# Windowed attention and SwiGLU on one core: fixed instruction orders, loads that cast, DMA transposes

## The chip, the cores and the metric

The kernel runs on one core of a Trainium2 chip. The metric is device time in microseconds (us), lower is better. Engines are named as in the profile: PE (matmuls; PEld its weight loads), DVE, ACT, POOL, and the queues SPq, ACTq and POOLq from which DMAs are issued. PSUM is the memory that PE writes its results to. The granted clock (row PEclk) is the share of PE's full clock that the profile shows. A casting load is a DMA that turns fp32 into fp16 on its way.

## The reference

```
scores = q @ k.T / sqrt(64)            # 8 sequences x 8 heads, 576 tokens, head size 64
scores = where(|i - j| <= 32, scores, -1e9)
x      = softmax(scores) @ v           # laid out as 4608 tokens x 512
out    = (silu(x @ w_gate) * (x @ w_val)) @ w_out      # 512 -> 1536 -> 512
```

Inputs and output are fp32; the kernels compute in fp16 with fp32 accumulation. Queries are taken in blocks of 64, each against 128 keys; a **pair** is two blocks (128 tokens, 36 pairs), its "scores" are the product with K and its "AV" the product with V, a **chunk** is 512 tokens (9 chunks), and a **stage** below is one chunk's FFN1 (12 units of 8 matmuls) and the FFN2 after it (48 matmuls) with four pairs of attention.

## The kernel before

The attention output of a pair is turned by PE and copied by DVE:

```python
def pair_xt(m):
    tp = ps_o.tile([128, GS, 128], FP16, tag="o", name="xt_ps")
    for g in range(GS):
        nc.tensor.transpose(out=tp[:, g, :], in_=x16[:, 128 * g:128 * g + 128], identity=ident)
    ...
    nc.vector.tensor_copy(out=xts[j][:, :, 128 * i4:128 * i4 + 128], in_=tp)
```

Weights come in fp32 slabs that ACT, DVE and POOL cast. The order within an engine is chosen by the compiler's scheduler.

## Time and profile before

| | before |
|---|---|
| time, median of 2 runs | 414.88 us |
| span of the profiled run | 413.3 us |
| first FFN1 matmul | 56.1 us |
| one steady stage, FFN1 start to FFN1 start | 38.85 us |
| PE busy | 358.0 us |

In the slices, each digit is a fortieth of the span. The prediction below shows those of PE, ACT and DMA, the chain of waits of the startup and one steady FFN2. One more pair of rows matters later: the copies of turned Q and K in before, from the page's groups (columns: line, engine, operation, out<-in, shapes, count, then busy us and mean ns of one, then idle time before).

```profile
L275 ACT ACTIVATE kT_106<-qk_ps 128x576 f16<-128x576 f16 x16 | 10.4, 648 | 7.9 <-DMA qst<-in_q_dram 6.4
L273 DVE COPY qB_109<-qk_ps 64x576 f16<-64x576 f16 x16 | 11.9, 744 | 2.8 <-PE qk_ps L267 2.7
```

A copy of 576 elements per partition takes 0.65 us on ACT and 0.74 us on DVE: 1.1 and 1.3 ns an element.

### The profile page before, as it was taken

What the parts mean: (1) busy time and instruction counts of PE and PEld (TensorE: products, weight loads), DVE (VectorE), ACT (ScalarE), POOL (GpSimd) and SP (SyncE); (2) the same over time, 40 slices, a digit from 0 to 9 for tenths busy, and PEclk for the clock granted to TensorE, in tenths of its full rate; (3) what the DMA queues carried; (4) which work ended last, traced back from release to release, by engine and by line L of the source; (5) the groups of instructions that cost most, each with busy time, mean ns of one, the idle gap of its engine ahead of it and who ended that gap; (6) DMA issues with size and microseconds to landing.
All of it is one profiled execution on the core that took longest, in us unless ns stands there. A gap on an engine that the chain in (4) does not pass through costs nothing.

```text
span 413.3 us, 6739 instructions
## 1 busy us (share of the span) xinstructions
PE 358.0 (87%) x2690; PEld 191.5 (46%) x2690; DVE 204.5 (49%) x338; ACT 173.0 (42%) x238; POOL 123.2 (30%) x181
## 2 busy tenths in 40 slices
PE   1210689958999999999999999999999999999994
PEld 0210544454546455554555555555455544544441
DVE  7332634664566464646646564566454633533300
ACT  2321335471455446344633373455436343533321
POOL 4562562856126231622353334133110000000000
PEclk9999999988999999999999999999999999999999
DMA  8999995975333523523363351301100100110022
GB/s 208 259 334 322 245 329 144 166 171 116 114 115 102 152 77 112 153 84 115 109 168 92 85 148 54 116 0 52 52 0 9 71 26 1 52 53 0 26 103 82
DMA packets 61862, 47.70 MB, mean 115 GB/s; under 512 B 39296, under 2 KB 55680, under 8 KB 61824
## 3 DMA queue, kind: packets, MB, share of 16 engines
q1 hardware_dynamic: 58880, 42.87, 38.3%
q10 hardware_dynamic: 2944, 4.33, 3.6%
q8 instruction: 23, 0.38, 0.4%
q14 instruction: 15, 0.12, 0.1%
HBM read 37.75 MB, written 9.44 MB: 114 GB/s over the span
## 4 chain that ended last, share of the span: by engine, by line
PE 78%; DMA 7%; ACT 6%; DVE 5%; SPq 2%; issue 1%; ACTq 0%
PE gv_ps L348 45%; PE ob L362 20%; DMA wst_t<-in_moe_w_gate_dram 5%; PE o_ps L314 4%; PE qk_ps L267 4%; ACT p_t L302 3%; PE s_ps L296 3%; PE xt_ps L332 3%; DVE p_t L305 1%; DMA qst<-in_q_dram 1%; SPq L233 1%; ACT ssb L354 1%; DVE xT L337 1%; ACT osb L370 1%; ACT L302 1%
## 5 line engine op out<-in xcount | busy, mean ns | idle before, releaser
L355 DVE TENSOR_TENSOR hT<-ssb,gv_ps 128x512 f16<-128x512 f16 x108 | 74.3, 688 | 101.6 <-ACT ssb L354 100.3
L354 ACT ACTIVATE ssb<-gv_ps 128x512 f16<-128x512 f32 x108 | 64.5, 597 | 128.4 <-PE gv_ps L348 128.4
L348 PE MATMUL gv_ps<-xT,wg_133 128*128 128x512 f16 x432 | 113.2, 385 | 0.9 <-DVE xT L337 0.5
L348 PE MATMUL gv_ps<-xT,wv_134 128*128 128x512 f16 x432 | 111.7, 381 | 0.0
L362 PE MATMUL ob<-wo_135,hT 128*128 128x512 f16 x432 | 102.0, 379 | 0.5 <-ACT osb L370 0.5
L348 PEld LDWEIGHTS <-wv_134 128*128 128x128 f16 x432 | 42.5, 98 | 51.6 <-issue 1.4
L348 PEld LDWEIGHTS <-wg_133 128*128 128x128 f16 x432 | 41.2, 99 | 46.2 <-issue 3.2
L362 PEld LDWEIGHTS <-hT 128*128 128x128 f16 x432 | 39.6, 98 | 40.4 <-issue 0.6
L370 ACT ACTIVATE osb<-ob 128x512 f32<-128x512 f32 x36 | 21.5, 596 | 55.4 <-PE ob L362 55.4
L257 POOL CAST v_122<-vS 64x512 f16<-64x512 f32 (+1 forms) x52 | 33.7, 648 | 29.7 <-PE o_ps L314 16.1
L257 POOL CAST v_112<-vS 64x512 f16<-64x512 f32 (+1 forms) x52 | 33.1, 638 | 30.8 <-PE o_ps L314 20.1
L302 ACT ACTIVATE p_t<-s_ps 128x1024 f16<-128x1024 f32 x36 | 36.7, 1025 | 12.7 <-PE s_ps L296 10.9
L305 DVE TENSOR_TENSOR p_t<-p_t,mask 128x1024 f16<-128x1024 f16 x36 | 28.1, 779 | 26.8 <-ACT p_t L302 26.6
L314 PEld LDWEIGHTS <-p_t 128*64 128x64 f16 x576 | 19.2, 117 | 14.2 <-issue 5.8
L337 DVE COPY xT<-xt_ps 128x512 f16<-128x512 f16 x36 | 15.1, 419 | 19.9 <-PE xt_ps L332 19.7
L296 PE MATMUL s_ps<-qB_109,kT_106 128*128 128x128 f16 x144 | 13.7, 239 | 10.9 <-ACT kT_106 L275 10.2
L296 PEld LDWEIGHTS <-kT_106 128*128 128x128 f16 x144 | 10.5, 108 | 14.5 <-ACT kT_106 L275 11.0
L314 PE MATMUL o_ps<-v_112,p_t 128*64 128x66 f16 x288 | 12.7, 209 | 3.6 <-DVE x_342 L323 1.2
L314 PE MATMUL o_ps<-v_122,p_t 128*64 128x66 f16 x288 | 11.8, 201 | 3.9 <-DVE x_793 L323 1.3
L296 PE MATMUL s_ps<-qB_119,kT_116 128*128 128x128 f16 x144 | 12.4, 232 | 2.7 <-ACT p_t L302 1.7
L275 ACT ACTIVATE kT_106<-qk_ps 128x576 f16<-128x576 f16 x16 | 10.4, 648 | 7.9 <-DMA qst<-in_q_dram 6.4
L273 DVE COPY qB_109<-qk_ps 64x576 f16<-64x576 f16 x16 | 11.9, 744 | 2.8 <-PE qk_ps L267 2.7
(348 smaller groups left out, 271.8 us busy)
## 6 DMA issues: line engine op xcount, KB each, us to landing
qst<-in_q_dram SPq DMA_DIRECT2D x32, 288.0 KB, 3.2
out_dram<-osb SPq DMA_DIRECT2D x36, 256.0 KB, 2.1
kst<-in_k_dram SPq DMA_DIRECT2D x28, 288.0 KB, 3.4
vS<-in_v_dram SPq DMA_DIRECT2D x24, 256.0 KB, 4.3
vS<-in_v_dram SPq DMA_DIRECT2D x16, 192.0 KB, 4.3
wst_t<-in_moe_w_val_dram ACTq DMA_DIRECT2D x4, 768.0 KB, 10.1
wst_t<-in_moe_w_gate_dram SPq DMA_DIRECT2D x4, 768.0 KB, 10.1
wost_t<-in_moe_w_out_dram SPq DMA_DIRECT2D x4, 768.0 KB, 8.5
```

What stands on the lines that cost most here:

```text
L257: nc.gpsimd.tensor_copy(out=o, in_=i)
L267: nc.tensor.transpose(out=ps[:, i, 96 * j:96 * j + 96], in_=t16[:, j, :, :], identity=ident[0:96, 0:96])
L296: nc.tensor.matmul(out=s[:, i, 128 * hp:128 * hp + 128], lhsT=kT[b % 2][:, hp, 64 * t:64 * t + 128], rhs=qB[b % 2][:, hp, :, 64 * t:64 * t ...
L302: nc.scalar.activation(out=p.rearrange("p a h q -> p (a h q)"), in_=s.rearrange("p a f -> p (a f)"), func=AF.Exp, bias=0.0, scale=1.0 / fl ...
L305: nc.vector.tensor_tensor(out=p, in0=p, in1=mask, op=ALU.mult)
L314: nc.tensor.matmul(out=o[64 * i:64 * i + 64, h // 4, 66 * (h % 4):66 * (h % 4) + 66], lhsT=p[:, i, h, :], rhs=v16[b % 2][:, t, h, :], star ...
L337: nc.vector.tensor_copy(out=xts[j][:, :, 128 * i4:128 * i4 + 128], in_=tp)
L348: nc.tensor.matmul(out=gv[:, i, :], lhsT=w[:, g, 128 * fk:128 * fk + 128], rhs=xts[j][:, g, :], start=(g == 0), stop=(g == GS - 1))
L354: nc.scalar.activation(out=ssb, in_=gv[:, 0, :], func=AF.Silu, bias=0.0, scale=1.0)
L355: nc.vector.tensor_tensor(out=hts[j][:, fk, :], in0=ssb, in1=gv[:, 1, :], op=ALU.mult)
L362: nc.tensor.matmul(out=ob, lhsT=hts[j][:, fk, 128 * sub:128 * sub + 128], rhs=wo16[:, fk, :], start=(fk == 0), stop=(fk == FKS - 1))
L370: nc.scalar.activation(out=osb, in_=ob, func=AF.Copy, bias=0.0, scale=1.0)
```

## The change

The intent: no engine's queue waits for a weight slab, and PE has less to do. Weights, V, and Q and K from the fourth sequence on are cast in the load (issued by POOL); Q and K of those sequences, and x of pairs 8 to 35, are turned by DMA. Q and K of the first three sequences are loaded in long runs and turned by PE. Scores use two half-height row tiles in place of a zero-padded Q. Every engine's order is fixed by hand. The core of it:

```diff
+    PARTS = ((0, 10), (320, 8))
+    fast.enter_context(tc.manual_schedule())
 ...
+    def turn_long(b, part, ks, qs):
+        t0, n = PARTS[part]
+        kd = kT[b % 2][:, :, 32 + t0:32 + t0 + 32 * n].rearrange("c h (p j) -> c j h p", j=n)
+        qd = qT[b % 2][:, :, t0:t0 + 32 * n].rearrange("c h (p j) -> c j h p", j=n)
 ...                                             # casts; n PE transposes for each of K and Q
+            cp(dst, ps[:, 0:n].rearrange("c j (h p) -> c j h p", p=32))
 ...
+    def turn_tok(b, tiles, dst, off):
+        for t0, n, st in tiles:
+            nc.sync.dma_start_transpose(
+                out=dst[:, :, off + t0:off + t0 + n], in_=st[0:n].rearrange("p h d -> p (h d)"))
 ...
-                nc.tensor.matmul(out=s[:, i, 128 * hp:128 * hp + 128], lhsT=kT[...128 rows...], rhs=qB[...128 columns...])
+                    for g in range(2):
+                        nc.tensor.matmul(out=s[:, g, i, hp, :], lhsT=kT[b % 2][64 * g:64 * g + 64, ...],
+                                         rhs=qT[b % 2][64 * g:64 * g + 64, ...])      # 64 columns
 ...
+    def x_dma(ms):
+        for m in ms:
+            x16 = x16s.pop(m).rearrange("p a h d -> p (a h d)")
+            nc.sync.dma_start_transpose(out=x_out(m), in_=x16)
 ...
+    def fetch(b):
+        load_v(b, range(5))                      # POOL: 5 casting loads
+        toks[b] = load_tok(k, b, "k16"), load_tok(q, b, "q16")       # 5 and 5 more
+        for t in (1, 3, 5, 7):
+            shift_v(b, t, cp_pool, cp_pool)
 ...
+    def ffn2(j, pairs):
+        scores(pairs[0:3])
+        ffn2_half(j, 0, 0); ffn2_half(j, 0, 1); ffn2_half(j, 1, 0)
+        avs(pairs[0:2]); scores(pairs[3:4]); x_dma(pairs[0:2])
+        ffn2_half(j, 1, 1); ffn2_half(j, 2, 0)
+        avs(pairs[2:4]); x_dma(pairs[2:4])
+        ffn2_half(j, 2, 1); ffn2_half(j, 3, 0); ffn2_half(j, 3, 1)
 ...
+    for j in range(1, NCH):                      # fetch(b) after unit 0 and place(b), its turning, after unit 9 of FFN1(j > 1)
```

(Lines are cut and joined here; the code is otherwise as in the change.)

## The prediction

> **What bounds the kernel now.** I read the page's slices first, then the chain of waits in order of time, then the timeline of one steady stage engine by engine, then busy time per stretch. The slices:
>
> ```profile
> PE   1210689958999999999999999999999999999994
> ACT  2321335471455446344633373455436343533321
> DMA  8999995975333523523363351301100100110022
> ```
>
> There are two regimes. For five slices (about 56 us) DMA is full and PE nearly idle; after that PE is full and nothing else is above seven tenths for long. The chain tells what the first regime waits for:
>
> ```profile
> 1.28 5.92 DMA qst<-in_q_dram
> ...
> 15.05 11.82 DMA wst_t<-in_moe_w_gate_dram
> 26.90 1.49 ACT wg_133 L251
> 28.41 10.61 DMA wst_t<-in_moe_w_gate_dram
> 39.06 1.36 issue
> 40.43 0.64 ACT kT_106 L275
> 41.12 0.73 PE s_ps L296 x5
> ...
> 56.11 4.27 PE gv_ps L348 x10
> ```
>
> This is the costliest flaw. The copy of the last head pair of K (kT, ACT, 40.43) needs only Q and K, which had landed and were cast by about 15 us. It stands in ACT's in-order queue behind casts of the gate weights, and these wait for 768 KB slabs. So some 25 us pass before the first full score matmul; then four pairs of blocks go through a chain of PE, ACT and DVE with little overlap, and FFN1 starts at 56.11.
>
> The second regime, PE in one FFN2 stage:
>
> ```profile
> 245.30 0.62 PE L296 MATMUL s_ps<-qB_119,kT_116 128*128 128x128 f16 x8
> 245.76 1.46 PE L362 MATMUL ob<-wo_135,hT 128*128 128x512 f16 x6
> 247.06 0.39 PE L332 MATMUL xt_ps<-ident,x_2710 128*128 128x128 f16 x4
> 247.37 0.60 PE L314 MATMUL o_ps<-v_122,p_t 128*64 128x66 f16 x16
> 247.91 1.47 PE L362 MATMUL ob<-wo_135,hT 128*128 128x512 f16 x6
> ```
>
> From start to start (one group's end overlaps the next): scores of a pair cost 0.46 us (8 matmuls), its AV 0.54 us (16, or 34 ns each), its x transposes 0.31 us, and six FFN2 matmuls 1.30 us, or 216 ns each. The chain shows the same 216 ns for FFN1: 80 matmuls in 17.28 us near the end, where nothing is mixed in. Within FFN1 there are also 12 transposes of Q and K per head pair: the timeline of 118 to 120 us has them between 118.63 and 119.14, 0.51 us. A stage of 512 tokens is then 144 x 0.216 = 31.1 us of FFN, 4 x 1.31 = 5.2 us of attention and 4 x 0.51 = 2.0 us of Q/K transposes, 38.3 us; the chain has 38.85 us from one FFN1 start to the next (175.41 to 214.26). So PE has under 1 us of holes per stage, and only less work on PE, or an earlier start, makes this kernel faster. Between 81.05 and 96.7 five pairs of attention stand alone, 15.6 us for 6.6 us of PE work: 9 us lost.
>
> **What the Trainium skill says.** "TensorE: Matmul & The Clock Gate", Part 3 (packing small matmuls), says that matmuls on different row groups run at the same time. The trace of before has no row-tiled matmul; its AV, split over column halves, starts one every 34 ns. "DMA: Bandwidth & Descriptors", SWDGE vs HWDGE vs iDMA, says that only GpSimd-issued DMAs can cast, and that GpSimd cores then compute each descriptor in software; "SBUF — State Buffer", SBUF: two separate sides, adds that some DVE modes lock GpSimd out while it writes them. No run here shows either yet: all loads are hardware queues q1 and q10. "Advanced Engine Details and Errata", X-Bar Transpose (TRN2), says that transposing DMAs are as fast as ordinary ones; not shown yet either.
>
> **The change, part by part.**
>
> *Startup.* Weights and V are cast in the load, so the weight casts leave ACT, DVE and POOL and nobody's queue waits for a slab. Q and K come in rows of up to 2560 B. Bytes needed before the first FFN1 matmul: Q, K and V of sequence 0, 3.5 MB, and one slab of each weight, 1.6 MB. At the 282 GB/s that the first 56.1 us show, 5.1 MB land by about 19 us. The chain, from durations of before at the slow clock of the startup: first K part landed at 6.5 us (in before the first 288 KB needed until 7.2); casts 1.3 (a 768-element ACT cast is 0.84), transposes 2 x 1.0, copies 2.5, scores of two pairs 2 x 1.0, exp 2 x 1.03, mask 0.7: about 18 us. The second part's casts, transposes and copies interleave, 3. Then AV 2 x 0.9, normalise 2 x 0.9, scores 2.0, exp 2.1, mask 0.7, AV 1.8, normalise 1.8, transposes and copies 1.5; partly overlapped I take 9 for these 13. FFN1 starts at **30 us** in place of 56: minus 26.
>
> *PE work after that start.* FFN unchanged: 1296 x 0.216 = 279.9 us. Attention of 32 pairs: scores become 16 half-height matmuls of 64 columns; at the 34 ns that AV needs for a load and a matmul of this width 0.55 us, plus AV 0.54, so 1.09 x 32 = 34.9 us (no gain over 0.46 unless the row tiles really overlap; what the form saves is the zero-padded Q tile and its two DVE copies of 0.75 us). x transposes stay on PE for pairs 4 to 7 only: 4 x 0.31 = 1.2; the other 28, 8.7 us with a DVE copy of 0.42 us each, go to DMA. Q/K transposes stay for sequences 1 and 2: 2 x 36 x 0.043 = 3.1 us, and five sequences (10 us) go to DMA. Sum **319.1 us**. In before the same sum is 279.9 + 32 x 1.31 + 7 x 2.05 = 336.2, and its span from 56.11 to the last matmul at 407.8 is 351.7: 15.5 us of holes.
>
> *Holes that remain.* The lone attention block of 15.6 us goes: two pairs run inside each of the first two FFN1s. But ACT there has two table loads of 1.28, two exps, copies and casts, some 7 us above its 0.6 per unit, with about 1.1 us of slack per unit and three PSUM buffers: 3 us lost each, **6**. In each of seven FFN2s the third score tile waits about 0.3 us for a PSUM buffer; and the last two pairs' x goes to xT by DMA. Their AV ends about 11 us into the stage, two normalisations (0.9 each) make the last transpose issue near 12.3, FFN1 wants it at 15, and DMAs of before land 2.1 (stores) to 4.3 us (V) after issue: between 0 and 1.6 us late. I take 1 us per stage, **7**. For the Q/K fetch and the rest, **4**. Total 17.
>
> *The tail.* The last store is split, its two copies on two engines: 0.3 of the 0.6 us copy, so 5.5 becomes about 5.
>
> Sum: 30 + 319.1 + 17 + 5 = 371 us of span; the timed runs are 1.6 above the span (414.88 to 413.3): **372 us**.
>
> **The rivals.** *(a) GpSimd's descriptors become the bound.* From the fourth sequence on each takes 15 casting loads of 128 to 256 KB in 256-byte pieces, up to 1024 pieces each. The engines carry this: in before 448 KB of V beside a 256 KB store took about 2 us of 16 engines, some 20 ns a piece, so 15 loads are about 18 us of a 40 us period. Descriptor generation in software has no row in the trace. At 2 us a load it is 30 us, hidden (the fetch can begin in the FFN2 before, when the older V is read out). At 5 us it is 75 us per sequence for five sequences: PE would wait over 35 us each time, and the kernel would be slower, 450 us or more. For it: 1024 software steps per load. Against: POOL loses its 66.8 us of V casts and its Q/K casts; an order fixed this carefully looks measured. I give it one in ten, with a mild form (some us per sequence, 380 to 390) besides. *(b) The DMA transposes are slow.* 28 of x and 50 of Q/K in one SP queue, with stores behind them. At 5 us each the x ones would put 3 to 5 us on each FFN1 start, 25 to 30 us in all: about 395. For it: the program order gives only 3 us. Against: 128 KB is half of a V load. *(c) Row-tiled scores do overlap* and a pair costs 0.3 us: 8 us less, about 362. *(d) Casting loads are slow at the start*: weights arrive below the 275 GB/s that FFN1 eats in its first pass (1.57 MB per three units of 1.73 us), so the gain moves from startup into FFN1(0): at half the rate some 10 to 15 us given back, 385.
>
> **Range and chances.** Even with (b) or (d) at their likely size the kernel stays ahead, as the startup alone is worth 26 us and its cause is plain in the chain. The low end takes (c) with no DMA stall and an FFN1 start at 25 us, 356; the high end takes (d) or half of (b), 392. Faster by over 2% 0.89, within 2% 0.04, slower 0.07, nearly all of it (a).
>
> **What would show it.** The first FFN1 matmul near 30 us; FFN1 starts 36 to 37 us apart from the third chunk on; scores at 0.5 us a pair from start to start; PE idle before FFN1 laid to a DMA transpose at about 1 us, not 4; no wait of the fourth to eighth sequence's scores on qT or kT. It is wrong if POOL's DMA rows fill its track, if matmuls of FFN1(0) wait for wg or wv, or if the exp table loads stall PE more than 3 us in the first two FFN1s.

## More of the kernel before

Q and K are loaded as fp32 and cast, then turned by PE into PSUM and copied out; the copies write rising addresses and read PSUM with a step:

```python
def prep_qk(b, hp, tiles, cq, ck):
    ps = ps_c.tile([128, 2, 1024], FP16, tag="c", name="qk_ps")
    ...                                        # cast, then 6 PE transposes of 96 tokens for each of Q and K
    qsrc = ps[:, 0, 0:S].rearrange("c (j p) -> c p j", j=J6)
    ...
    nc.vector.tensor_copy(out=qd[0:64, hp, 0], in_=qsrc[0:64])      # qd is "c ... p j": j runs fastest, as in memory
    nc.vector.tensor_copy(out=qd[64:128, hp, 1], in_=qsrc[64:128])
    nc.scalar.activation(out=kd, in_=ksrc, func=AF.Copy, bias=0.0, scale=1.0)
```

## The result, and the profile after

| | before | after |
|---|---|---|
| time, median of 2 runs | 414.88 us | 434.0 us |
| span of the profiled run | 413.3 us | 431.9 us |
| first FFN1 matmul | 56.1 us | 39.1 us |
| start of the third FFN1 (chunk 2) | 136.7 us | 148.3 us |
| PE busy | 358.0 us | 340.4 us |

The ratio is 1.0446, 95% interval 1.0375 to 1.0516: slower. Ratios here are the mean time of one kernel's fast runs over that of the other's of the same rounds, so not quite the ratio of the medians.

PE is busy for 18 us less and FFN1 starts 17 us earlier, and yet the kernel is 19 us slower. The slices of the page after:

```profile
PE   0337966579689499939993999599959999998993
ACT  0783366664766134512352236234523533363320
PEclk9999988999979799978998899999989999999998
DMA  9999941348019990699059903993699031013002
```

Set beside the PE row of before, this one has two new kinds of holes: a ragged stretch from the sixth to the thirteenth slice (54 to 140 us), and then a dip in every fourth slice or so, until the last two stages. Beside the dips DMA stands at 9, and beside four of the five the clock row has a 7 or 8.

**The ragged stretch.** The chain of waits after, in the startup (columns: start us, us, what):

```profile
2.23 8.44 DMA qs<-in_q_dram
...
13.65 1.26 PE t_ps L256 x10
14.94 5.85 DVE qT L238
20.83 0.62 PE s_ps L279 x16
```

The copy of turned Q takes 5.85 us where the prediction allowed 2.5 for a K and a Q copy together. By form, all twelve such copies:

```profile
L238 DVE COPY qT<-t_ps 128x1280 f16<-128x1280 f16 x3 | 17.6, 5856 | 8.4 <-PE t_ps L256 8.4
L235 ACT ACTIVATE kT<-t_ps 128x1280 f16<-128x1280 f16 x3 | 17.6, 5855 | 1.1 <-PE t_ps L256 1.1
L235 ACT ACTIVATE kT<-t_ps 128x1024 f16<-128x1024 f16 x3 | 14.2, 4724 | 3.0 <-PE t_ps L256 3.0
L238 DVE COPY qT<-t_ps 128x1024 f16<-128x1024 f16 x3 | 14.1, 4695 | 5.1 <-PE t_ps L256 5.1
```

That is 4.6 ns an element, on both engines alike, against 1.1 and 1.3 in before.

**The dips.** The chain around the start of the third FFN1, and of the last one:

```profile
138.76 0.70 DVE x L315
139.46 0.42 SPq L338
139.98 8.27 DMA xT<-x
148.24 0.09 issue
148.33 22.91 PE gv_ps L348 x96
...
391.14 2.44 DMA xT<-x
393.57 0.25 issue
393.82 20.88 PE gv_ps L348 x96
```

The last x transpose of the stage lands 8.27 us after its issue in the one, and 2.44 us after it in the other; and the FFN1 that follows takes 22.91 us in the one, 20.88 us in the other. In the list of PE's waits (us in total, times, longest) this is the first line:

```profile
PE gv_ps L348 <- DMA xT<-x: 27.3, 6, 6.7
```

The busy time of the engines in stretches of 2 us in the first shows both (columns: stretch, length, busy us and instructions of PE, PEld, DVE, ACT and POOL, then the granted clock, the DMA engines' share and GB/s; a share above 1 means that packets overlap in the count):

```profile
138.00:140.00 2.00, 2.00 (x11) 0.91 (x10) 1.42 (x3) 0.60 (x1) 2.00 (x3) 1.00 2.67 119
140.00:142.00 2.00, 1.86 (x9) 0.66 (x7) 0.00 (x0) 0.06 (x1) 2.00 (x3) 1.00 1.93 187
142.00:144.00 2.00, 0.00 (x0) 0.00 (x0) 0.00 (x0) 1.82 (x2) 1.96 (x4) 1.00 1.89 192
144.00:146.00 2.00, 0.00 (x0) 0.00 (x0) 0.00 (x0) 0.00 (x0) 1.83 (x4) 0.91 2.51 145
146.00:148.00 2.00, 0.00 (x0) 0.00 (x0) 0.00 (x0) 0.00 (x0) 1.82 (x4) 0.50 1.59 180
148.00:150.00 2.00, 1.67 (x5) 0.58 (x6) 0.00 (x0) 0.00 (x0) 1.94 (x4) 0.50 1.45 259
154.00:156.00 2.00, 2.00 (x11) 0.92 (x10) 0.69 (x1) 0.87 (x2) 0.00 (x0) 1.00 2.06 156
```

PE is idle from about 142 on, the clock falls to 0.50 before FFN1 begins and stays there into it, and POOL and DMA are busy all along. POOL's timeline tells with what:

```profile
135.31 4.20 POOL L206 DMA_DIRECT2D k<-in_k_dram  x5
139.45 4.25 POOL L206 DMA_DIRECT2D q<-in_q_dram  x5
```

These are the casting loads of the *next* sequence, up to 1024 pieces of 256 bytes each. They stand behind unit 0 of the following FFN1 in the program, but POOL's order binds only POOL: it runs ahead as soon as its buffers are free, and so reaches the DMA engines in the very us in which the x transposes are issued. In the last two stages there is nothing left to fetch, and no dip.

### The profile page after: what moved, and what is told of

The parts are those of the page before. It is cut to its first block, busy times and chain, and to the rows that moved or that the text cites. A ratio compares the mean times of both kernels' runs of the same rounds, so it can differ in the third digit from the quotient of the medians.

```text
span 431.9 us, 6717 instructions
## 1 busy us (share of the span) xinstructions
PE 340.4 (79%) x2686; PEld 171.2 (40%) x2686; DVE 173.8 (40%) x268; ACT 186.3 (43%) x226; POOL 122.8 (28%) x168
## 4 chain that ended last, share of the span: by engine, by line
PE 64%; DMA 13%; DVE 8%; issue 6%; ACT 6%; SPq 1%; ACTq 0%; DVEq 0%
PE gv_ps L348 44%; PE ob L367 15%; DMA xT<-x 10%; DVE qT L238 2%; DMA qs<-in_q_dram 2%; PE o_ps L304 2%; ACT ssb L354 2%; PE s_ps L279 2%; ACT p_t L285 2%; DVE x L315 2%; PE t_ps L256 1%; DVE hT L356 1%; ACT kT L235 1%; DMA ks<-in_k_dram 1%; DVE t L238 1%
## 5 line engine op out<-in xcount | busy, mean ns | idle before, releaser
L348 PE MATMUL gv_ps<-xT,wg 128*128 128x512 f16 (+1 forms) x480 | 121.7, 379 | 39.7 <-DMA xT<-x 27.3
L356 DVE TENSOR_TENSOR hT<-ssb,gv_ps 128x512 f16<-128x512 f16 (+1 forms) x120 | 76.0, 634 | 180.7 <-ACT ssb L354 180.7
L354 ACT ACTIVATE ssb<-gv_ps 128x512 f16<-128x512 f32 (+1 forms) x120 | 67.1, 560 | 162.0 <-PE gv_ps L348 162.0
L348 PE MATMUL gv_ps<-xT,wv 128*128 128x512 f16 (+1 forms) x480 | 120.1, 375 | 0.0
L367 PE MATMUL ob<-wo,hT 128*128 128x512 f16 x432 | 99.2, 384 | 0.0
L215 POOL DMA_DIRECT2D v<-in_v_dram x40 | 33.7, 850 | 188.5 <-PE s_ps L279 91.9
L348 PEld LDWEIGHTS <-wg 128*128 128x128 f16 x480 | 47.9, 101 | 92.3 <-issue 52.4
L348 PEld LDWEIGHTS <-wv 128*128 128x128 f16 x480 | 48.8, 102 | 52.0 <-issue 10.0
L285 ACT ACTIVATE p_t<-s_ps 128x1024 f16<-128x1024 f32 x36 | 34.9, 1023 | 13.5 <-PE s_ps L279 13.4
L241 POOL COPY v<-v 64x512 f16<-64x512 f16 x60 | 36.9, 615 | 7.6 <-DMA v<-in_v_dram 4.6
L238 DVE COPY qT<-t_ps 128x1280 f16<-128x1280 f16 (+1 forms) x6 | 31.7, 5276 | 13.5 <-PE t_ps L256 13.5
L279 PEld LDWEIGHTS <-kT 64*128 64x128 f16 x576 | 11.0, 98 | 19.0 <-issue 13.4
```

The costliest lines, as they stand in the source:

```text
L215: nc.gpsimd.dma_start(out=v16[b % 2][p0:p0 + hi - lo, 2 * m, :, 0:D], in_=vb[lo:hi])
L238: nc.vector.tensor_copy(out=o, in_=i)
L241: nc.gpsimd.tensor_copy(out=o, in_=i)
L279: nc.tensor.matmul(out=s[:, g, i, hp, :], lhsT=kT[b % 2][64 * g:64 * g + 64, hp, 64 * t:64 * t + 128], rhs=qT[b % 2][64 * g:64 * g + 64, h ...
L285: nc.scalar.activation(out=p.rearrange("p g i h q -> p (g i h q)"), in_=s.rearrange("p g i h q -> p (g i h q)"), func=AF.Exp, bias=0.0, sc ...
L348: nc.tensor.matmul(out=gv[:, i, 0:n], lhsT=w[:, g, 128 * fk:128 * fk + 128], rhs=xts[j][:, g, lo:lo + n], start=(g == 0), stop=(g == GS - 1))
```

## The experiments

Two causes are to be told apart: **A**, the strided copies, and **B**, the collision of the x transposes with the fetch. The first four ran on one chip (before: 414.62 us there), the other three on another (before: 415.19 us); across chips, the ratios to before are the safer comparison.

**e1_copy: the copies alone.** Same elements, written in the order of addresses:

```diff
-        kd = ....rearrange("c h (p j) -> c j h p", j=n)      # and qd
+        kd = ....rearrange("c h (p j) -> c h p j", j=n)
-            cp(dst, ps[:, 0:n].rearrange("c j (h p) -> c j h p", p=32))
+            cp(dst, ps[:, 0:n].rearrange("c j (h p) -> c h p j", p=32))
```

> Only the twelve copies of turned Q and K out of PSUM are changed: same elements, but written in the order of rising addresses (read with a stride) in place of written with a step of 16 or 20 bytes. Theory A (the strided write makes them slow): each falls from 5.3 and 4.7 us to about 1.3, FFN1 starts about 8 us earlier, the first two FFN1s and the first FFN2 lose some 15 us more of PE holes, 434 becomes 406 to 414; the waits of FFN1 for xT in the later stages stay at 6 to 8 us. Rival A2 (the two engines slow each other, or PSUM reads are what is slow): the copies stay near 5 us and the time within 1%.

Measured: 420.57 us, ratio to before 1.0154 (1.0120 to 1.0188). (The 5.3 us in the expectation is the mean of both sizes; the longer copies take 5.86.) The copies, asked for by their tile (shortest, median and longest in ns, first and last start, forms):

```profile
L235 ACT ACTIVATE kT<-t_ps x6: 1015/1120/1228, 13.6 to 107.7; 128x1280 f16<-128x1280 f16 x3, 128x1024 f16<-128x1024 f16 x3
L238 DVE COPY qT<-t_ps x6: 1224/1358/1492, 15.0 to 108.5; 128x1280 f16<-128x1280 f16 x3, 128x1024 f16<-128x1024 f16 x3
```

Both engines are at 1.0 to 1.5 us, though they still work at the same time and now read PSUM with a step. So the strided write was the cost; rival A2 falls. Why such a write is slow is not tested further (see the last section). The gain, 13.4 us, is smaller than I expected: FFN1 starts 7 us earlier and the third FFN1 14 us earlier (134.05 us), but part of the ragged stretch remains (see e6). The waits for xT stay, as expected.

**e2_xpe: x by PE.** `x_dma` of pairs 8 to 35 is replaced by four PE transposes and a DVE copy, with the FFN2 halves as before:

```diff
-            x_dma(pairs[0:2])
-            x_dma(pairs[2:4])
+            x_pe_a(pairs[0:1])          # after avs(pairs[2:4]); PSUM tiles from the pool of three
+            x_pe_a(pairs[1:2])          # after ffn2_half(j, 2, 1)
+            x_pe_a(pairs[2:4])          # after ffn2_half(j, 3, 0)
```

> Only x of pairs 8 to 35 is turned by PE and a DVE copy again in place of the DMA transpose; Q and K still go by DMA. Theory B (the x transposes queue behind the next sequence's casting loads, PE waits and its clock falls): FFN1-to-FFN1 periods of 41 to 44 us fall to about 37, no stretch at clock 0.5 after the third FFN1, 434 becomes 403 to 410. Rival B2 (PE is slowed by something else of the fetch, e.g. SBUF traffic or late K/Q): periods stay above 40 and the time above 425.

Measured: 396.08 us, ratio 0.9551 (0.9535 to 0.9568), 37.9 us less than the 434.0 of the change. The chain, two FFN1s in a row:

```profile
178.76 20.73 PE gv_ps L357 x96
214.48 20.73 PE gv_ps L357 x96
```

The stage is 35.72 us and each FFN1 is at full speed, while the fetch goes on as it did. So the fetch does not slow PE; rival B2 falls. My saving was too small, in part because I had set the undisturbed stage at 37.

**e3_gate: the fetch held back.** x, Q and K are all turned by DMA as in the change; only the first casting load of each later sequence waits for the first Silu of its FFN1:

```diff
-                ffn1_unit(j, u)
+                a = ffn1_unit(j, u)
-                        fetch(fetched)
+                        fetch(fetched, a)       # first load of fetch: after(i, a)
```

> Only the start of each later sequence's casting loads is moved: the first waits for the first Silu of the FFN1 in which it stands in the program, in place of starting in the FFN2 before. Everything is still turned by DMA. Theory B (collision): x transposes land about 2.4 us after issue in all stages, the wait for xT falls to about 2.5 us and the clock holds, saving 20 us or more, 410 to 416, unless Q and K then come late, which would show as waits of scores for qT. Rival B3 (transposes with K/Q work nearby are slow of themselves): landing stays at 5 to 8 us and the time within 1.5%.

Measured: 402.90 us, ratio 0.9704 (0.9656 to 0.9752), 31.1 us less than the change and below the range I had expected. From issue to landing of the x transposes, in the change and then here (shortest, median, longest):

```profile
DMA to landing us min/median/max: 2.4/5.5/8.4
```

```profile
DMA to landing us min/median/max: 2.4/2.4/3.8
```

No transfer was removed, only moved, and the delay is gone: it was the collision, not the transposes; rival B3 falls. Which part that the two share is the narrow one, the runs do not tell. Here Q and K come a little late, as the list of PE's waits in this run shows (us in total, times, longest):

```profile
PE gv_ps L351 <- DMA xT<-x: 5.1, 5, 1.6
PE s_ps L282 <- DMA qT<-q: 3.9, 3, 2.2
```

**e4_copy_xpe: e1 and e2 together.**

> Both: copies in order of addresses, x by PE. If the causes A and B are separate, the savings add: 378 to 388, and this is faster than the kernel before (415). If one hides the other, over 395.

Measured: 381.52 us, ratio 0.9201 (0.9181 to 0.9220). The two savings, 13.4 and 37.9, sum to 51.3; together they give 52.5. A and B are separate.

**e5_copy_gate: e1 and e3 together.**

> Copies in order of addresses, and the later fetches held back to their FFN1, x still by DMA. If the effects add as they did with x on PE: 402.9 less 13 to 14, 388 to 391, so x on PE is worth 7 to 9 us more than x by an undisturbed DMA. If the late Q and K then bind in full, over 394.

Measured: 389.77 us, ratio 0.9383 (0.9323 to 0.9443), as expected. With x by DMA even undisturbed, the ratio is 0.018 above that of e4, some 7.5 us. PE's waits here are 5.4 us for qT beside 5.1 us for xT, so the late Q has a part in it.

**e6_early: what was left of the ragged stretch.** In e4 PE idles in the first FFN1 from about 49 us, as Q of sequence 1 lands at 52.7 us behind loads that nobody needs yet:

```diff
-        if u == 2:
+        if u == 0:
             s1p0 = seq1_load(0, a)
-        if u == 5:
+        if u == 3:
             s1p1 = seq1_load(1, a)
-            load_wo(0, 2); load_wo(1, 2)        # moved: after unit 0 of the second FFN1, and waiting for it
```

> e4_copy_xpe with sequence 1's Q and K allowed two FFN1 units earlier and the out weights, needed only at 100 us, held back until the second FFN1. Theory: the hole of about 6 us before the ninth to tenth unit of the first FFN1 (Q landing at 52.7 us behind 3.1 MB of out weights) closes, with the slow clock after it: 372 to 377. Rival: the bound there is ACT and DVE work, not the landing: within 1% of 381.5.

Measured: 376.83 us, ratio 0.9084 (0.9052 to 0.9117); e4, on the other chip, had 381.52 us and 0.9201. Two things were moved at once, so which of them did it is not shown. The clock row has no dip left:

```profile
PEclk9999999999999999999999999999999999999998
```

**e7_filler: the clock.** The change, with 24 matmuls that nobody reads put in the five waits:

```diff
         ffn2_half(j, 3, 1)
+        if n and j < 6:
+            fl = ps_o.tile([128, 512], FP32, tag="o", name="fill")
+            for r in range(24):
+                nc.tensor.matmul(out=fl, lhsT=hts[j][:, r % 12, 0:128], rhs=wo16[:, r % 12, :], start=True, stop=True)
```

> The changed kernel with 24 matmuls that nobody reads (5.2 us at full clock) put at the end of those five FFN2s after which PE waits 6 to 8 us for xT. If the low clock in the following FFN1 comes from PE standing idle: these FFN1s take 20.7 to 21 us in place of 22.6 to 23.4, and the time falls by 7 to 11 us, 423 to 427, though PE does 26 us more work. If the low clock comes from anything else: no change or up to 10 us slower.

Measured: 427.78 us, ratio 1.0287 (1.0229 to 1.0345): 6.2 us less than the change, just outside what I had expected; the intervals of the two ratios do not overlap. In the chain the landing is as late as ever, but the FFN1 after it runs at full speed:

```profile
185.84 8.19 DMA xT<-x
194.28 20.89 PE gv_ps L348 x96
```

Four of the five took 20.73 to 20.89 us, with the fetch going on beside them: the slow FFN1s follow from PE's idleness, not from the traffic. The first still took 22.58 us: PE was idle for 2.43 us before it, and the granted clock was 0.51 in its first 2 us; an idle time of 2.27 us before another (236.71) left that one at 20.89. "TensorE: Matmul & The Clock Gate", Part 1 of the Trainium skill, says that an idle window of about 3.4 us halves the clock. The trace of the change agrees: PE is idle from 141.86 us, and the clock is down before 146 us. The 2.43 us of e7 are shorter than the page's window, so here a shorter wait was enough once; how short it may be is not settled.

## Why the prediction was wrong

The prediction was 372 us with faster at 0.89; measured were 434.0 us, slower. Slower had a chance of 0.07, nearly all of it for rival (a), which did not come about. Step by step:

**Startup: the direction right, one term mis-sized.** The diagnosis of before (copies stuck behind weight casts) holds, and FFN1 does start 17 us earlier; but at 39.1 us, not 30. The term that failed is "copies 2.5": one K and one Q copy of a part in series stood for some 2.5 us, and one copy alone takes 5.86. At the rates of before's copies it would be 1.4 to 1.7 us. I had not looked at the order of the write: before steps through the source, the change steps through the destination. With that mended (e1) FFN1 starts at 32.1 us. That this is near the 30 is partly luck: the first Q part landed at 10.7 us, not at 6.5, so the other terms together were some 2 us too large.

**The first two FFN1s.** The same term counts again for sequences 1 and 2. The terms of the prediction put the start of the third FFN1 at 112.5 us: 30, four FFN passes of 62.2, eight pairs at 1.09, 1.2 and 3.1 of transposes, 7.3 of holes. Measured: 148.3. Of these 36 us the copies are 14.3 (e1, 134.05), x by PE another 5.2 (e4, 128.85), the late Q 4.9 (e6, 123.97). The rest, some 11 us, was not told apart by a run; "3 us lost each" for ACT in the first two FFN1s was too low: in e6 PE is still idle for 5.4 us between 50 and 64 us, within the first of them, while the chain goes mostly through ACT; and the chain of e6 also waits for ACT's casts in the first FFN2 (1.27 and 1.06 us).

**The step that cost most: "between 0 and 1.6 us late. I take 1 us per stage".** The slack was right: the stage without a fetch on either side takes 36.46 us (357.36 to 393.82), within the 36 to 37 predicted, and its x lands in 2.4 us. (There is luck in how well it fits the terms, 31.1 + 4 x 1.09 + 1: scores came 0.28 us a pair cheaper, and PE still waited 1.35 to 1.70 us for x.) The step that failed is the landing time: "2.1 (stores) to 4.3 us (V)" became 6.0 to 8.4 us beside a fetch, and PE waited 4.4 to 6.7 us. I took it from before's trace, where the DMA engines carry little (a busy share of 0.16 from 240 to 330 us); beside the fetch the share was 1.6 to 2.7. The stages from the third FFN1 on take 43.6, 44.1, 41.9, 41.0 and 38.4 us, 26.7 us more than five of 36.46. Of this, 10.3 us is slow FFN1s (22.91, 23.28, 23.43, 22.58 and 22.58 against 20.89), and most of the rest is waiting.

**I held the fact and did not use it.** Rival (a) says that the fetch "can begin in the FFN2 before", as a reason why POOL would be in time. From the same passage it follows that its 15 loads then fall on the us in which x must pass. Rival (b) asked only whether a DMA transpose is slow by itself; it is not (e3). The size that it gave, 25 to 30 us, is close to the 26.7 measured, but that is chance: the cause it gave was another. The halved clock after a wait was in none of the rivals. One sum in rival (d) is also wrong: 1.57 MB per three units of 1.73 us are 303 GB/s, not 275; nothing here hung on it.

**What held.** PE's work, by the undisturbed stage. Rival (a): a casting load costs POOL 0.69 to 0.96 us by its size, not 2 or 5. Rival (d): during the startup no matmul of the first FFN1 waits for wg or wv in the list of PE's waits. Rival (c) is true: the row tiles do overlap. Three pairs of scores in the change:

```profile
128.78 0.81 PE s_ps L279 x48
```

That is 0.27 us a pair, against 0.46 in before and the 0.55 that I took; over 36 pairs that is some 7 us saved against before, which the two causes above outweighed. "TensorE: Matmul & The Clock Gate", Part 3, had said so, and this trace agrees.

## What to carry to other kernels

Before a DMA is put into a chain with a few us of slack, list what else its engines carry at that moment: an order within one queue does not hold the other queues back, and a load that is freed early by an early buffer is a load that collides. Cost a copy by the step of its write as well as by its element count, and keep the fastest dimension of a strided rearrangement on the destination (shown here for fp16 copies out of PSUM). Where PE may wait for some us, count the half-speed stretch after the wait too: here waits of 4.4 to 6.7 us were followed by FFN1s 1.7 to 2.5 us longer.

## What the Trainium skill lacked or had wrong

- "Advanced Engine Details and Errata", SBUF Cachelines, names 16-byte lines and "Different cacheline per access: performance penalty", without a size. Here 2-byte writes with a step of 16 or 20 bytes took 4.6 ns an element on ACT and DVE alike, and in address order 0.96 to 1.2 ns (e1). That the lines are the reason is the page's account; the runs show only the order of the write.
- "Advanced Engine Details and Errata", X-Bar Transpose (TRN2), says that transposing DMAs are as fast as ordinary ones. Alone, 128 KB landed in 2.4 us, and a 256 KB store in 2.6 (median); these sizes do not test the rate. The section gives no time for the company: beside casting loads the same transpose took up to 8.4 us.
- "DMA: Bandwidth & Descriptors", SWDGE vs HWDGE vs iDMA, gives no time per descriptor. Here a casting load of 1024 pieces held POOL for 0.88 to 0.96 us, one of 512 for 0.69 to 0.77.
- "TensorE: Matmul & The Clock Gate", Part 3, gives row-tiling speedups for wide matmuls. Here 16 half-height matmuls of 64 columns took 0.27 us, where 8 of full height and 128 columns took 0.46.
